# Layer 2's first rows loaded and normalized among the last sums of layer 1

## The chip, the cores and the metric

The kernel runs on one core of one Trainium2 chip. The metric is the device time of one execution in microseconds. The engines are named as in the profile: PE (TensorE: matmuls and transposes, PEld its weight loads), DVE (VectorE), ACT (ScalarE), POOL (GpSimd) and SP (SyncE, which here only issues DMAs). Each engine executes its own queue in order and waits on semaphores; a DMA issued by an engine stands in that engine's queue like any other instruction, so that an issue that has to wait holds back what stands behind it.

## The reference

```python
x = A_x                                   # (1, 2048, 640) fp32
x = x + _A_ref(_layernorm(x), A_wqkv, A_wo)
x = x + _B_ref(_layernorm(x), dft_seq_re, dft_seq_im, dft_hid_re, dft_hid_im)
x = x + _A_ref(_layernorm(x), A_wqkv, A_wo)
x = x + _B_ref(_layernorm(x), dft_seq_re, dft_seq_im, dft_hid_re, dft_hid_im)

def _A_ref(x, wqkv, wo):                  # 32 heads of 20 columns
    q, k, v = split((x @ wqkv))           # no masks, no biases
    p = softmax(q @ k.T * 20 ** -0.5)
    return (p @ v).reshape(1, 2048, 640) @ wo

def _B_ref(x, Cs_re, Cs_im, Ch_re, Ch_im):   # real part of a DFT over both axes
    a, b = x @ Ch_re.T, x @ Ch_im.T
    return Cs_re @ a - Cs_im @ b
```

A layer is attention with its residual sum, then the Fourier block with its own; there are two layers with the same weights.

## The kernel before, in words

All matrices are fp32; a product of two fp32 matrices is made of three matmuls of high and low parts. `split` (L110 to L115) makes them: ACT writes the high part (L114), DVE the low part as the difference (L115). `three` (L117) and `passes` (L124) issue the three matmuls. Rows of x are handled in blocks of 128.

The order of the work is written out by hand: a manual schedule, where each engine receives its instructions in the order in which the program text issues them. Memory comes from pools on the left or right side that are opened and closed as the program goes on.

A layer runs through these classes:

- `Qkv`. `load(k)` (L171 to L175) fetches two row blocks, 2k and 2k+1, with DMAs on SP, one for each block for k of 0 and 1, and one for both otherwise. `stats(k)` calls `moments` (L137 to L151): for each of the two blocks two BATCH_NORM_STATS2 and one BATCH_NORM_AGGREGATE on DVE (L145, L146), then four small steps on POOL (L147 to L150), which make scale and bias of the rows. `norm(k)` applies them on ACT (L154), two instructions. `turn(tb)` transposes four row blocks on PE, 20 transposes (L192), and splits them into `xt`. `fetch` (L200) loads a chunk of the weights for queries or keys, `weights` splits it. `prologue` (L262) puts these together, then goes through the four groups of rows: `product` (30 matmuls into `pqk` for queries and 30 for keys), `keep`, `norms`, `value`.
- `Attention` runs over the heads and takes most of the span; `Check`, which looks at the DFT matrices for their symmetries, stands among its work. `Project` multiplies by wo and adds the first residual; it stores the rows to the scratch tensor d_x[0].
- `Fourier`. `accumulate(m)` sums over the sequence ("pacc" matmuls); the rows are folded by symmetry, and the sixteen sums follow `ORDER = (0, 1, 4, 5, 2, 6, 3, 7, 8, ..., 15)`. `hidden(t)`, t from 0 to 7, makes the product along the columns ("phid" matmuls, 18 of them), then the difference and the sum of its two halves (ACT L1150, DVE L1151 and L1152), adds them to the residual rows (L1160, L1161: the lower rows on DVE, the upper ones on POOL), and stores row blocks t and t+8 with one DMA on SP (L1182, called store t below). For t of 0 and 2 some one-row copies on POOL come with it (L1176, L1181). `residual(t)` (L1157) issues the load of those rows on POOL's queue into one of four buffers. In `run` (L1184), hidden(0) to hidden(3) stand behind accumulate(11) to accumulate(14), hidden(4) to hidden(7) behind the last sum; residual(4) to residual(6) follow accumulate(12) to accumulate(14), and residual(7) follows hidden(4), whose buffers and those of the tiles ahead it needs free.

At the change of layers, layer 2's load(k) reads row blocks 2k and 2k+1, and store t of layer 1 writes row blocks t and t+8: load(0) needs stores 0 and 1, load(1) stores 2 and 3, load(2) stores 4 and 5, load(3) stores 6 and 7. In before, all four loads stand on SP behind store 7. In the prologue of before, ACT's order is norm(0), weights' high parts, norm(1), then the transposes' high parts; DVE's order is the statistics of x0 and x1, the weights' low parts, statistics of x2, the transposes' low parts. x0 is the tile that load(0) fills, and so on; the rows of the profile call all of them "xa".

A general path for matrices without the symmetries exists; it is not executed with these inputs.

Of the kernel before, what the change touches and what calls it, by code (L numbers as in the profile page):

```python
# [5 lines left out]
F32 = mybir.dt.float32  # L6
# [12 lines left out]
LAYERS = 2  # L19
ND = D // 128  # L20
# [15 lines left out]
def mha_fnet_kernel(ctx, tc, x_in, wqk, wv, wo, seq, hid, nat_seq, nat_hid, out):  # L36
# [66 lines left out]
    def rows(ap, t, n=1):  # L103
        return ap[t * 128:(t + n) * 128].rearrange("(n p) d -> p n d", p=128)
# [55 lines left out]
    class Qkv:  # L160
# [6 lines left out]
            s.made, s.raw = set(), {}  # L167


        def load(s, k):  # L170

            s.xn[k] = s.room(f"x{k % 4}", [2, D], F32, "xa")
            n = 1 if k < 2 else 2
            for i in range(0, 2, n):
                nc.sync.dma_start(s.xn[k][:, i:i + n], rows(s.src, 2 * k + i, n))  # L175

        def stats(s, k):
            s.rs[k] = moments(s.xn[k], 2, "a")
# [16 lines left out]
                s.xt[tb, dc] = [x[:, 0], x[:, 1]]  # L195
                split(x[:, 0], x[:, 1], p)

        def fetch(s, c, room=None):
            s.raw[c] = (room or s.fill)("wraw", [ND, 128], F32, "wraw")
            nc.sync.dma_start(s.raw[c], wqk[c])  # L200

        def weights(s, w, c, vector):
# [56 lines left out]
            else:  # L259
                A.activation(dst, src, AF.Copy)  # L260

        def prologue(s, vals, xt, fill, room, att):  # L262
            s.xtp, s.fill, s.room = xt, fill, room
# [7 lines left out]
            raw = [vals(f"v{NT - 1 - dc}", [HD], F32, "wvraw") for dc in range(ND)]  # L271
            for dc in range(ND):
                nc.sync.dma_start(raw[dc], wv[dc, :, :HD])
# [12 lines left out]
            s.stats(3)  # L286
            s.wv = fill("wv", [ND, 2, HD], F32R, "wv")
            for dc in range(ND):
                split(s.wv[:, dc, 0], s.wv[:, dc, 1], raw[dc])

            def ones(t):
                s.v[t] = vals(f"v{t}", [H * VW + 12], F32, "v")
# [709 lines left out]
    class Fourier:  # L1002
# [160 lines left out]
        def hidden(s, t):  # L1163
            lo, hi = s.x[t][:, 0], s.x[t][:, 1]
            o = (t % 4) * 128
            s.nb += 2
            p = [bank(f"b{(s.nb + i) % 8 if t >= NQ else 6 + i}", [128, 512], "phid")[:, :HD + 2] for i in range(2)]
# [12 lines left out]
            if t in (0, 2):  # L1180
                G.tensor_copy(hi[0:1], m)  # L1181
            nc.sync.dma_start(pair(s.dst, t), s.x[t])  # L1182

        def run(s):  # L1184
            s.x, s.acc, s.nb = {}, {}, 0
            for i, m in enumerate(s.ORDER):
                tb, ri, q = m // 8, (m // 4) % 2, m % 4
# [3 lines left out]
                s.parts(i + s.AHEAD)  # L1191
                if m in (6, 7, 9, 10):
                    s.middle((6, 7, 9, 10).index(m))
                if 11 <= m < 15:
                    s.hidden(m - 11)
                if m < 8 and ri == 1:
                    s.residual(q)
                elif 12 <= m < 15:
                    s.residual(m - 8)
            for t in range(4, NP):  # L1200
                s.hidden(t)
                if t == 4:
                    s.residual(NP - 1)

        def general(s):

# [47 lines left out]
    def layer(L, src, dst, general):  # L1254

        tag = f"{L}g" if general else f"{L}"
        q = Qkv(tag, src)
        q.flag = near[:, 5 + L:6 + L] if general else near[:, L:L + 1]
        a = Attention(q, tag)
        p = Project(a, src, d_x[0])  # L1260
        f = Fourier(p, d_x[0], dst, check)
        f.tag = tag
        vals, xt = Pool(f"v{tag}"), Pool(f"xt{tag}", "right")
        fill = Pool(f"fill{tag}", "right")
        a.kq = Pool(f"kq{tag}")
        room = Pool(f"pro{tag}")
        banks(f"q{tag}")
        q.prologue(vals, xt, fill, room, a)
        room.close()

        room = a.room = check.room = Pool(f"att{tag}")
        banks(f"a{tag}")
# [15 lines left out]
        if general:  # L1288
            a.general(done, p)
        else:  # L1290
            a.run(done, p, tasks[L])
        room.close()
        a.kq.close()
        vals.close()
# [4 lines left out]
        p.run()  # L1299
        room.close()  # L1300
        p.late.close()
        if not general:
            f.own = Pool(f"four{tag}")
            f.run()
            f.own.close()
        f.keep.close()
        f.late.close()
        if general:
            f.general()

    def layers(general):
        for L in range(LAYERS):
            layer(L, x_in if L == 0 else d_x[1], out if L == LAYERS - 1 else d_x[1], general)

# [74 lines left out]
```

## Time and profile before

| | us |
|---|---|
| three runs | 2577.2, 2580.96, 2582.15 (median 2580.96) |
| the profiled execution | 2581.92 |
| its span | 2580.1 |
| mean granted clock of TensorE | 0.993 |
| PE busy | 2516.4 (98% of the span) |
| ACT busy | 2136.1 (83%) |
| DVE busy | 982.2 (38%) |
| POOL busy | 539.2 (21%) |

The runs are single executions; the profiled one carries the trace. Busy time counts instructions that do work, not waits and issues of DMAs. In a row of the timeline stand the start and the time in microseconds, the engine, the line, the operation, output and inputs, partitions and elements, the count, and in brackets the idle time before it with what ended it. A row of the chain of waits has the start, the time and the piece of work. SPq means SP's DMA queue.

### The profile page before, as it was taken

The page shows a single profiled execution, that of the slowest core. Times are in us where ns is not written, and L with a number is a line of the kernel's source. Part 1 is how long each engine was busy: PE and PEld are TensorE (multiplying, and loading weights), DVE is VectorE, ACT ScalarE, POOL GpSimd, SP SyncE. Part 2 cuts the span into 40 slices and gives each one's busy share as a digit, 9 for nine tenths or more (in the row PEclk, how much of TensorE's full clock was granted, in tenths as well). Part 3 has the DMA queues.
Part 4 walks back from the last instruction along what each step waited for, and adds up shares of the span by engine and source line. Part 5 has one row for each costly group of instructions (what it writes and reads, how often), then busy time and mean ns, then how long its engine had stood idle before and what let it go on. Part 6 is the DMA issues. An engine that isn't in the chain of part 4 may idle for free.

```text
span 2580.1 us, 43634 instructions
## 1 busy us (share of the span) xinstructions
PE 2516.4 (98%) x16350; PEld 1159.2 (45%) x16350; DVE 982.2 (38%) x2081; ACT 2136.1 (83%) x2429; POOL 539.2 (21%) x1068
## 2 busy tenths in 40 slices
PE   7999999999999999999889999999999999999997
PEld 6644444443333332249775444444433333322596
DVE  5244422344333333416662444223332323242275
ACT  5687899988999999975255888999899999999752
POOL 2112111112111111214420221111121111121143
PEclk9999999999999999999989999999999999999999
DMA  4233221222323223326552342222222222133364
GB/s 170 96 96 114 87 86 45 79 96 75 104 67 90 80 88 108 122 88 235 188 182 92 103 127 83 67 61 73 81 81 65 65 61 80 53 87 104 106 241 162
DMA packets 124921, 263.84 MB, mean 102 GB/s; under 512 B 28080, under 2 KB 52432, under 8 KB 124700
## 3 DMA queue, kind: packets, MB, share of 16 engines
q1 hardware_dynamic: 83804, 150.61, 18.1%
q0 software_dynamic: 40896, 110.34, 13.6%
q8 instruction: 132, 2.16, 0.4%
q14 instruction: 89, 0.73, 0.1%
HBM read 176.60 MB, written 84.21 MB: 101 GB/s over the span
## 4 chain that ended last, share of the span: by engine, by line
PE 89%; DVE 4%; DMA 2%; POOL 2%; issue 1%; ACT 1%; SPq 0%; DVEq 0%; ACTq 0%; POOLq 0%
PE acc L494 37%; PE psc L483 27%; PE pqk L127 11%; PE pv L127 6%; PE py L120 2%; PE py L122 2%; PE py L121 2%; PE pn L227 1%; PE ptr L192 1%; DVE of L501 1%; DMA xd<-d_x 1%; DMA craw<-in_seq_dram 1%; POOL xd L1161 0%; DVE ot L508 0%; DVE on L506 0%
## 5 line engine op out<-in xcount | busy, mean ns | idle before, releaser
L486 ACT ACTIVATE e<-psc 128x1024 f32<-128x1024 f32 x2048 | 1937.8, 1122 | 164.5 <-PE psc L483 128.1
L494 PE MATMUL acc<-e,v 128*32 128x512 f32 x8192 | 1061.5, 602 | 3.8 <-DVE of L501 3.3
L483 PE MATMUL psc<-stq,stk 62*128 62x512 f32 x4096 | 815.2, 462 | 4.6 <-ACT e L486 3.0
L483 PEld LDWEIGHTS psc<-stq,stk 62*128 62x128 f32 x4096 | 341.4, 184 | 836.6 <-ACT e L486 789.9
L494 PEld LDWEIGHTS acc<-e,v 128*32 128x32 f32 x8192 | 187.5, 108 | 366.2 <-issue 338.7
L515 POOL DMA_DIRECT2D o<-oh x256 | 131.2, 521 | 989.6 <-DVE oh L510 988.3
L127 PE MATMUL pqk<-xt,wqk 128*128 128x512 f32 x1200 | 317.6, 409 | 6.1 <-DVE top L228 4.4
L127 PEld LDWEIGHTS pqk<-xt,wqk 128*128 128x128 f32 x1200 | 217.7, 190 | 91.7 <-issue 37.3
L501 DVE STREAM_TRANSPOSE of<-acc 128x512 f32<-128x512 f32 x64 | 45.8, 716 | 529.2 <-PE acc L494 529.2
L112 DVE CAST hl<-pqk 128x512 fp32r<-128x512 f32 x64 | 44.2, 691 | 427.4 <-PE pqk L127 427.4
L127 PE MATMUL pv<-wv,xt 128*128 128x320 f32 x960 | 159.8, 317 | 0.0
L127 PEld LDWEIGHTS pv<-wv,xt 128*128 128x128 f32 x960 | 140.9, 188 | 26.0 <-issue 21.5
L515 POOL DMA_DIRECT2D o<-ot x256 | 128.3, 509 | 0.8 <-issue 0.2
L222 POOL DMA_DIRECT2D scrq<-hl x40 | 28.4, 710 | 386.6 <-DVE hl L115 264.2
L726 DVE TENSOR_REDUCE far<-cq 128x1 f32<-128x512 f32 (+5 forms) x169 | 98.6, 584 | 5.7
L120 PE MATMUL py<-wo,o 128*128 128x320 f32 x320 | 99.1, 310 | 1.4 <-DVE xr L908 1.4
L121 PE MATMUL py<-wo,o 128*128 128x320 f32 x320 | 98.6, 308 | 0.0
L122 PE MATMUL py<-wo,o 128*128 128x320 f32 x320 | 98.6, 308 | 0.0
L730 DVE TENSOR_TENSOR cq<-cq 128x512 f32<-128x512 f32 (+4 forms) x166 | 96.3, 580 | 2.7 <-DMA cq<-in_nat_seq_dram 2.4
L222 POOL DMA_DIRECT2D scrk<-hl x40 | 28.0, 701 | 295.2 <-DVE hl L115 249.8
L258 DVE COPY v<-pv 128x320 f32<-128x320 f32 x32 | 15.7, 490 | 183.5 <-PE pv L127 183.5
L228 DVE TENSOR_REDUCE top<-pn 32x1 f32<-32x512 f32 x80 | 53.4, 675 | 30.4 <-PE pn L227 30.4
(193 smaller groups left out, 1749.9 us busy)
## 6 DMA issues: line engine op xcount, KB each, us to landing
cq<-in_nat_seq_dram POOLq DMA_DIRECT2D x64, 512.0 KB, 5.3
scrq<-hl POOLq DMA_DIRECT2D x40, 512.0 KB, 3.2
scrk<-hl POOLq DMA_DIRECT2D x40, 512.0 KB, 3.5
stq<-scrq SPq DMA_DIRECT2D x256, 80.0 KB
stk<-scrk SPq DMA_DIRECT2D x128, 160.0 KB
o<-o SPq DMA_DIRECT2D x16, 1280.0 KB
stq<-scrq SPq DMA_DIRECT2D x256, 40.0 KB
stk<-scrk SPq DMA_DIRECT2D x128, 80.0 KB
```

The lines of the kernel that those rows point to most:

```text
L120: PE.matmul(out_ap, ah, bh, start=start, stop=False)
L121: PE.matmul(out_ap, ah, bl, start=False, stop=False)
L122: PE.matmul(out_ap, al, bh, start=False, stop=stop)
L127: yield lambda i=i, j=j, k=k: PE.matmul(out_ap, a[i], b[j], start=dc == 0 and k == 0, stop=dc == ND - 1 and k == 2)
L222: G.dma_start(s.scr["qk"[k]][c * 128:(c + 1) * 128, :, tb * 512:(tb + 1) * 512], hl.bitcast(F32))
L483: PE.matmul(p[:, i], s.k[g, kc // 8, j][r, kc % 8 * 128:(kc % 8 + 1) * 128], s.q[g, qb, j][r], start=True, stop=True)
L486: A.activation(e, p, AF.Exp, scale=SCALE)
L494: PE.matmul(s.acc[32 * j:32 * j + 32], s.a.v[kc][:, v0:v0 + 32], s.e[n, j // 2][:, j % 2], start=kc == 0, stop=kc == NT - 1, skip_group_ch ...
L501: V.transpose(t0.rearrange("p b c -> p (b c)"), s.acc)
L515: G.dma_start(s.o[k, h * DH:(h + 1) * DH, qb * 512:(qb + 1) * 512], hl[k][32 * j:32 * j + DH])
L726: V.tensor_reduce(to, x, op=OP.max, axis=AX.X, apply_absolute_value=True)
L730: V.tensor_tensor(y, x, y, op=op)
```

## The change

- A generator `Qkv.begin` takes over the first part of the prologue in three steps: it issues load(0), load(1) and the two weight chunks (on SP) and places the raw weights for v; then stats(0) and stats(1); then norm(0) and norm(1). The weight chunks go into the tiles "k3" and "k4" of the attention's pool of keys and queries, x0 and x1 into a pool of their own, `first`.
- `Fourier.run` gets this generator for the next layer: the loads and the statistics are issued behind the last sum and ahead of hidden(4), the normalization behind hidden(5). For that, `keep` is closed there, and the pool `four` is placed on the right side.
- hidden(3) moves from behind accumulate(14) to directly behind hidden(2), ahead of accumulate(14), and uses the banks b0 and b1.
- The rest of the prologue stays where it was. Its load(2) and load(3) are issued on ACT's queue instead of SP's in layer 2 and stay on SP in layer 1. In both layers norm(1) now stands ahead of the weights' splits.

In the built order, SP has layer 2's loads of x0 and x1 and both weight chunks between store 3 and store 4; DVE has the statistics of x0 and x1 ahead of hidden(4)'s sums; POOL has the two chains of scales ahead of hidden(4)'s adds; ACT has norm(0) and norm(1) behind the second tile's copy (hidden(5)), then hidden(6) and hidden(7), load(2), which waits for store 5, load(3), which waits for store 7, and only then the weights' and the transposes' high parts. PE's transposes of x0 and x1 stand directly behind hidden(7).

```diff
-        def load(s, k):
+        def load(s, k, queue=nc.sync):
-            s.xn[k] = s.room(f"x{k % 4}", [2, D], F32, "xa")
+            s.xn[k] = (s.first if k % 4 < 2 else s.room)(f"x{k % 4}", [2, D], F32, "xa")
...
-                nc.sync.dma_start(s.xn[k][:, i:i + n], rows(s.src, 2 * k + i, n))
+                queue.dma_start(s.xn[k][:, i:i + n], rows(s.src, 2 * k + i, n))
...
+        def begin(s, first, kq, vals):
+            s.first = first
             for k in range(2):
                 s.load(k)
-            s.fetch(0)
-            s.fetch(ND, room)
+            s.fetch(0, kq, "k3")
+            s.fetch(ND, kq, "k4")
+            s.wvraw = [vals(f"v{NT - 1 - dc}", [HD], F32, "wvraw") for dc in range(ND)]
+            yield
+            for k in range(2):
+                s.stats(k)
+            yield
+            for k in range(2):
+                s.norm(k)
+            yield
+
+        def prologue(s, vals, xt, fill, room, att, begin):
+            s.xtp, s.fill, s.room = xt, fill, room
+            next(begin, None)
             for k in (2, 3):
-                s.load(k)
+                s.load(k, nc.sync if s.src is x_in else nc.scalar)
...
-            s.stats(0)
-            s.norm(0)
-            s.stats(1)
+            for _ in begin:
+                pass
             for k in range(2):
                 s.weights(w[k], k * ND, False)
-            s.norm(1)
             s.stats(2)
             s.turn(0)
...
-        def run(s):
+        def run(s, after):
...
-                if 11 <= m < 15:
+                if 11 <= m < 14:
                     s.hidden(m - 11)
+                if m == 13:
+                    s.hidden(3)
...
+            s.keep.close()
+            after = after()
+            for _ in range(2):
+                next(after, None)
             for t in range(4, NP):
                 s.hidden(t)
                 if t == 4:
                     s.residual(NP - 1)
+                elif t == 5:
+                    next(after, None)
...
+    class Start:
+        def __init__(s, L, src, general):
...
+            s.vals, s.a.kq, s.first = Pool(f"v{tag}"), Pool(f"kq{tag}"), Pool(f"first{tag}")
+            s.begin = s.q.begin(s.first, s.a.kq, s.vals)
...
-            f.own = Pool(f"four{tag}")
-            f.run()
+            f.own = Pool(f"four{tag}", "right")
+            f.run(after)
             f.own.close()
```

More of the change, by code (lines that the diff above doesn't have):

```diff
@@ L1166, in hidden @@
             s.nb += 2
-            p = [bank(f"b{(s.nb + i) % 8 if t >= NQ else 6 + i}", [128, 512], "phid")[:, :HD + 2] for i in range(2)]
+            p = [bank(f"b{(s.nb + i) % 8 if t >= NQ else i if t == 3 else 6 + i}", [128, 512], "phid")[:, :HD + 2] for i in range(2)]
             for ri in range(2):
@@ L1262, in layer @@
         f.tag = tag
-        vals, xt = Pool(f"v{tag}"), Pool(f"xt{tag}", "right")
-        fill = Pool(f"fill{tag}", "right")
-        a.kq = Pool(f"kq{tag}")
+        xt, fill = Pool(f"xt{tag}", "right"), Pool(f"fill{tag}", "right")
         room = Pool(f"pro{tag}")
         banks(f"q{tag}")
-        q.prologue(vals, xt, fill, room, a)
+        q.prologue(vals, xt, fill, room, a, start.begin)
         room.close()
+        start.first.close()
         room = a.room = check.room = Pool(f"att{tag}")
@@ L1290, in layer @@
         else:
-            a.run(done, p, tasks[L])
+            a.run(done, p, tasks)
         room.close()
@@ L1301, in layer, with after @@
         p.late.close()
-        if not general:
-            f.own = Pool(f"four{tag}")
-            f.run()
+        if general:
+            f.keep.close()
+            f.late.close()
+            f.general()
+        else:
+            f.own = Pool(f"four{tag}", "right")
+            f.run(after)
             f.own.close()
[L1306 to L1309, printed above, removed]
+            f.late.close()
     def layers(general):
+        todo = [Start(0, x_in, general)]
+        next(todo[0].begin)
         for L in range(LAYERS):
-            layer(L, x_in if L == 0 else d_x[1], out if L == LAYERS - 1 else d_x[1], general)
+            last = L == LAYERS - 1
+            def after():
+                if last:
+                    return iter(())
+                todo.append(Start(L + 1, d_x[1], general))
+                return todo[-1].begin
+            layer(todo[L], d_x[1] if L else x_in, out if last else d_x[1], general, tasks[L], after)
+            if general and not last:
+                next(after())
     layers(False)
```

22 lines of the change are left out of this document (10 added, 12 removed).

## The prediction

> **What bounds the kernel now.** I read the head of the page and its chain of waits first, then the windows over the change of layers, then the chain and the timeline there.
>
> ```profile
> span 2580.1 us, 43634 instructions
> PE 2516.4 (98%) x16350; PEld 1159.2 (45%) x16350; DVE 982.2 (38%) x2081; ACT 2136.1 (83%) x2429; POOL 539.2 (21%) x1068
> PE 89%; DVE 4%; DMA 2%; POOL 2%; issue 1%; ACT 1%; SPq 0%; DVEq 0%; ACTq 0%; POOLq 0%
> ```
>
> PE is busy for 98% of the span and holds 89% of the chain, so a change that leaves the matmuls as they are can only win where PE stands idle. The windows (busy us of PE, PEld, DVE, ACT, POOL, then the granted clock, the DMA share and GB/s) show where that is:
>
> ```profile
> 1260.00:1270.00 10.00, 10.00 (x57) 8.74 (x57) 4.88 (x10) 0.88 (x2) 8.37 (x10) 1.00 0.60 201
> 1270.00:1280.00 10.00, 10.00 (x62) 8.91 (x61) 7.82 (x15) 2.44 (x5) 6.30 (x8) 1.00 0.83 271
> 1280.00:1290.00 10.00, 2.85 (x20) 2.58 (x18) 5.01 (x10) 0.88 (x2) 5.20 (x6) 0.85 0.89 303
> 1290.00:1300.00 10.00, 1.43 (x3) 0.55 (x4) 6.38 (x16) 4.61 (x6) 2.72 (x8) 0.50 1.02 379
> 1300.00:1310.00 10.00, 10.00 (x44) 8.88 (x45) 9.21 (x23) 7.96 (x15) 3.59 (x22) 0.79 0.48 168
> ```
>
> PE works 4.3 of the 20 us from 1280 to 1300; those 15.7 us are all that the change can go after. The chain (start, us, who) says what fills them:
>
> ```profile
> 1267.91 0.72 POOL xd L1181
> 1268.64 2.81 DMA d_x<-xd
> ...
> 1278.32 6.37 DMA xd<-d_x
> ...
> 1284.82 1.05 POOL xd L1160
> 1285.87 1.07 POOL xd L1161
> 1286.95 0.36 SPq L1182
> 1287.41 4.04 DMA xa<-d_x
> 1291.47 0.90 DVE ast L145 x2
> 1292.39 0.21 DVE amv L146
> ...
> 1298.32 1.64 ACT xa L154 x2
> 1300.00 3.88 PE ptr L192 x17
> 1303.88 7.02 PE pqk L127 x30
> 1310.91 2.36 PE ptr L192 x20
> ```
>
> The last residual load (6.37) ends in POOL's adds and in store 7 at 1286.95. All of layer 2's loads stand behind that store on SP, so only then come the load (4.04), statistics, normalization, transposes, and at 1303.88 the stream of 30 pqk matmuls at 7.02/30 = 0.234 us. That stream is the yardstick: behind it PE has no hole left.
>
> **Part by part, at the change of layers.** hidden(3) goes ahead of accumulate(14), whose nine matmuls are 9 x 0.234 = 2.1 us. POOL, though, is in hidden(2)'s copies until 1267.91 + 0.72 = 1268.6, and then needs its two adds:
>
> ```profile
> 1270.53 0.92 POOL L1160 TENSOR_TENSOR xd<-xd,r 128x321 f32<-128x321 f32 x1 [1.24 <-DVE r L1152]
> 1271.41 1.12 POOL L1161 TENSOR_TENSOR xd<-xd,r 128x319 f32<-128x319 f32 x1
> ```
>
> That is 2.0 us (1270.53 to 1272.53), so store 3 is issued at about 1270.65, 1.9 earlier than the 1272.53 of before. Row blocks 0 to 3 are what stores 0 to 3 write, and the second half of x1 waits for store 3 to land. A store's landing is not shown alone but for the 2.81 above; the load's 4.04 bounds it on the other side. I take 3.6, nearer the upper one since the DMA share is 0.83 here: the last half of x1 is issued at 1274.25. By then store 3, two residual loads and x0, x1 have to pass: 0.655 x (1 + 2 + 2) = 3.28 MB. At the 379 GB/s of the row at 1290 that is 8.65 us.
>
> ```profile
> 1290.85 0.95 SPq L175 DMA_DIRECT2D xa<-d_x  x2
> ```
>
> Counted from 0.95 behind store 3's issue (two issues on SP, as in this row), x1 has landed at 1271.6 + 8.65 = **1280.3**. The ends: 1278.3 if only the 4.04 of a load counts, 1282.0 if the raw weights queued behind (two chunks, 0.655 MB, 1.7 us) share the way.
>
> Here is the price. DVE executes in order, and the statistics of x0 and x1 stand in its queue ahead of hidden(4)'s sums. Before, those came at
>
> ```profile
> 1275.38 0.49 DVE L1151 TENSOR_TENSOR r<-phid,r 128x322 f32<-128x322 f32 x1 [1.40 <-ACT r L1150]
> ```
>
> Now they wait for 1280.3 plus one row block's statistics, 0.90 + 0.21 = 1.1: 1281.4, **6.0 late**. Queued behind on DVE are hidden(5) to hidden(7); POOL is held too, since the two small chains of the row scales stand ahead of hidden(4)'s adds:
>
> ```profile
> 1293.69 0.22 POOL L147 TENSOR_SCALAR ars<-amv 128x2 f32<-128x2 f32 x1 [6.76 <-DVE amv L146]
> ...
> 1295.11 0.19 POOL L150 TENSOR_TENSOR ars<-ars 128x2 f32<-128x2 f32 x1
> ```
>
> One chain is 1.6 us (1293.69 to 1295.30), so POOL is at hidden(4) at 1283.0 and done 2.0 later. Only behind these adds does POOL issue residual(7), at 1285.1 instead of 1278.32 (+6.8). Its landing is 5.7 by the median of the view of DMA issues, 6.37 in the chain above:
>
> ```profile
> xd<-d_x POOLq DMA_DIRECT2D x16, 640.0 KB, 5.7
> ```
>
> With 5.7 and the adds' 1.05 + 1.07, store 7 is issued at 1285.1 + 5.7 + 2.1 = **1292.9** against 1286.95. DVE's own share, four tiles of some 2.3 us (from the first sum at 1275.38, 0.49 each, and the adds), ends at about 1290.5 and is hidden under that.
>
> What is gained: x0 and x1 are normalized long before (the 1.64 of ACT at 1298.32 leaves the path), and their 20 transposes (17 of them 3.88) run while store 7 lands. But loads 2 and 3 now stand on ACT's queue, the second one waiting for store 7's landing, and behind it on ACT are the weights' high parts and the copies of the transposes. So ACT stands still until 1292.9 + 3.6 = 1296.5, issues (0.48), and then come:
>
> ```profile
> 1296.97 1.35 ACT L114 ACTIVATE wqk<-wraw 128x640 fp32r<-128x640 f32 x2
> ...
> 1297.73 1.56 DVE L115 TENSOR_TENSOR wqk<-wraw,wqk 128x640 fp32r<-128x640 f32 x2 [1.95 <-ACT wqk L114]
> ...
> 1302.85 0.69 DVE L115 TENSOR_TENSOR xt<-ptr,xt 128x512 fp32r<-128x512 f32 x1 [0.16 <-ACT xt L114]
> ```
>
> First weight on ACT 0.7 (half of 1.35), both low parts on DVE 1.56: 1299.3. In DVE's queue stand next the statistics of x2, 2 x 1.11 = 2.2, then the first low part of the transposes, 0.69: the second pqk matmul starts at 1302.2. Before it started at 1303.88 + 0.23 = 1304.1: **-1.9**. x2 itself waits only for store 5 and is there by then (store 5 near 1288, then 3.6 and a load's 4.04: 1295.6).
>
> The clock takes that back. Before, the stream came right behind the transposes:
>
> ```profile
> 1300.69:1304.10 3.41, 3.41 (x16) 3.33 (x16) 2.96 (x6) 2.38 (x5) 1.34 (x4) 0.50 0.05 17
> ```
>
> This window has a clock of 0.50 and holds transposes but for two matmuls at its end, and the stream after it runs at full rate (7.02 for 30). In the changed kernel the transposes are long over and PE has stood still when the stream begins, so it starts at half rate, as it did here:
>
> ```profile
> 218.57 3.68 PE L127 MATMUL pqk<-xt,wqk 128*128 128x512 f32 x8 [2.24 <-DVE top L228]
> ```
>
> 0.46 us each instead of 0.234. From the window's length of 3.4 us, a full one has passed after 3.4 to 6.8 us, on average 5.1: eleven matmuls at +0.23 are +2.5 (ends +1.7 and +3.4). Boundary: -1.9 + 2.5 = **+0.6**. The Trainium skill, "TensorE: Matmul & The Clock Gate", "Part 4: PE-mode transpose", says that transposes do not count as a busy PE for the clock. The row at 1300.69 speaks against it, since the clock opened behind transposes alone; by the page the stream of before would be cold as well, the 2.5 would fall on both kernels, and the sum below would be -1.5 instead of +1.0.
>
> **Part by part, elsewhere.** Layer 1's start runs through the same code with its norm(1) now ahead of the weights on ACT:
>
> ```profile
> 12.00 0.90 POOL L149 TENSOR_SCALAR ars<-amv 128x2 f32<-128x2 f32 x1
> 12.98 0.62 POOL L150 TENSOR_TENSOR ars<-ars 128x2 f32<-128x2 f32 x1
> 13.64 1.73 ACT L154 ACTIVATE xa<-xa,ars 128x640 f32<-128x640 f32 x2 [1.05 <-POOL ars L150]
> ```
>
> Those two POOL steps took 0.24 and 0.19 in the next chain; without DVE's splits beside them norm(1) starts up to 1.1 earlier, 12.5, and ends 14.3. Weights follow (1.35, low part to about 16.5), x2's statistics 2.2, the first low part 0.7: 19.4. Before, the stream's second matmul stood at about 19.5, behind transposes. So -0.2 at best, up to +1 for queueing and up to +1.7 for a later opening of the clock: ends -0.2 and +2.7, I take +0.8, near the best end because the transposes still run close ahead. At the very end:
>
> ```profile
> 2563.05 7.16 DMA xd<-d_x
> ```
>
> the last load of layer 2 meets less traffic, hidden(3) and its store being 1.9 earlier: between 0 and 7.16 - 6.37 = -0.8, taken as -0.4. The attention, the projection and the sums over columns keep their instructions, and the pools' places cost nothing that a row could show: 0.
>
> **Sum.** +0.6 + 0.8 - 0.4 = **+1.0**, on the profiled execution's 2581.92 us (span 2580.1 and 1.8 around it). That execution is 1.0 above the median of 2580.96, so 2582.9 there is **2582.0** on the median's footing. A difference of 0.2% is 5.2 us, about what a measurement of this kernel can tell from none (its three runs lie 4.95 apart): faster is below 2575.8, slower above 2586.1.
>
> **The rivals.**
>
> *The early rows cost hidden(4) nothing* (faster). If x0 and x1 land before DVE wants hidden(4)'s sums, store 7 goes out at 1286.95 as before, lands 1290.6, and the stream's second matmul is due 5.9 earlier than I have it, 1296.3; PE then stands still for less long, the half rate costs about 2.4, and the boundary gives 1296.3 - 1304.1 + 2.4 = -5.4, in all -5.0, and -6.0 with the start at its good end: 2575 to 2576, on the edge of what counts as faster. It decides at x1's landing by 1274.3 (1275.38 less 1.1). For it: DMA was only 0.60 busy from 1260 to 1270. Against: x1's last half is issued at 1274.25 by my own count. A mix of the good ends gets nearly as far: x1 at 1278.3 (-2.0), clock at its good end (-0.8), start -1.0, tail -0.4: 2577.8. Chance 0.15.
>
> *Two cold or late prologues* (slower). Each microsecond that x1 lands behind 1280.3 moves hidden(4), residual(7), store 7 and the stream by one. From 1284.3 on the whole is more than 5.2 slower. Price: landing at 1285, because the four residual and row loads in flight share the engines with three stores and the weights, gives +4.7 + 1.0, about +6; the half rate over the whole stream of 30 (30 x 0.23 = 6.9 instead of 2.5) gives +4.4 more on its own, +5.4; the start at its bad end adds 1.9. About 2588. For it: DMA share 0.83 to 1.02 here, and DVE, POOL and ACT each wait in order for something of another engine. Against: 379 GB/s was reached in the busiest window. Chance 0.22.
>
> *The clock counts no transposes.* Then the stream of before would be as cold, the 2.5 falls on both, and the sum is -1.5: 2579.5. The full rate of that stream speaks against it; 0.03 of the forecast's chance, and no change of side.
>
> *It does not do what it says.* The loads might stand behind store 7 after all; but in the built order SP has them between store 3 and store 4. If they landed late anyway, that is the case above.
>
> **How the numbers follow.** The forecast has 0.63, the faster case 0.15, the slower 0.22. Eight in ten reach from the good case, 2576, to the bad one, 2588; the forecast's own range, from its terms' ends, is 2577.8 to 2586. Faster 0.15, same 0.63, slower 0.22.
>
> **What would show it.** Right: BATCH_NORM_STATS2 around 1279 to 1281 ahead of hidden(4)'s sums, which start at about 1281.4; residual(7) near 1285; store 7 near 1293; an empty ACT until 1296.5; pqk matmuls of 0.46 for some 5 us. Wrong: sums of hidden(4) still at 1275 or 1276, or a store 7 before 1288 (then faster), or x1 landing after 1284 (then slower), or a stream at full rate from its start.

## The result: 8.0 us slower, and where they are lost

The changed kernel takes 2588.13 us (median of 9 runs, 2585.01 to 2590.28), the kernel before 2580.15 (9 runs, 2576.39 to 2582.28). The ratio is 1.0032, with a 95% interval of 1.0022 to 1.0043. The forecast was 2582.0, +1.0, with a range that ended at 2586. The profiled execution took 2586.92 us, with a span of 2585.0.

The windows of the changed kernel, to be laid beside those of before (busy us of PE, PEld, DVE, ACT, POOL, then clock, DMA share, GB/s):

```profile
1270.00:1280.00 10.00, 10.00 (x60) 8.63 (x59) 5.01 (x7) 2.44 (x5) 2.92 (x4) 1.00 0.88 298
1280.00:1290.00 10.00, 4.18 (x29) 3.91 (x27) 7.39 (x19) 3.90 (x5) 5.24 (x11) 0.94 0.43 162
1290.00:1300.00 10.00, 3.98 (x20) 3.74 (x20) 6.42 (x9) 0.44 (x1) 5.46 (x7) 0.67 0.89 282
1300.00:1310.00 10.00, 1.25 (x2) 0.75 (x3) 4.59 (x11) 3.79 (x7) 0.82 (x2) 0.50 1.02 382
1310.00:1320.00 10.00, 9.55 (x44) 7.73 (x44) 8.86 (x23) 7.75 (x15) 4.39 (x32) 0.86 0.14 48
```

PE's hole was 15.7 us between 1280 and 1300. It is now 20.6 us between 1280 and 1310 (30 less 4.18, 3.98 and 1.25). DVE's row for 1270 to 1280 names the reason: 5.01 us busy instead of 7.82, though it has the statistics added. It stands still and waits for rows. Its timeline:

```profile
1269.59 2.28 DVE L1171 TENSOR_TENSOR xd<-xd,r 128x321 f32<-128x321 f32 x1
...
1279.14 0.89 DVE L145 BATCH_NORM_STATS2 ast<-xa 128x6 f32<-128x320 f32 x2 [3.82 <-DMA xa<-d_x]
...
1282.60 0.89 DVE L145 BATCH_NORM_STATS2 ast<-xa 128x6 f32<-128x320 f32 x2 [2.33 <-DMA xa<-d_x]
...
1283.69 0.89 DVE L145 BATCH_NORM_STATS2 ast<-xa 128x6 f32<-128x320 f32 x2
...
1284.73 0.83 DVE L145 BATCH_NORM_STATS2 ast<-xa 128x6 f32<-128x320 f32 x2
...
1285.73 0.44 DVE L1162 TENSOR_TENSOR r<-phid,r 128x322 f32<-128x322 f32 x1
```

The last row is hidden(4)'s first sum, at 1285.73 instead of 1275.38. Its product was ready long before (the copy on ACT starts at 1276.24, below); DVE idled 3.82 and 2.33 us for the two halves of x0. x1's halves came about a microsecond apart behind it: the last was there when DVE came to it at 1284.73 (its semaphore counts full at 1284.5 in the trace). The chain of waits takes it from there:

```profile
1273.31 9.26 DMA xa<-d_x
1282.60 0.90 DVE ast L145 x2
...
1289.45 6.36 DMA xd<-d_x
1295.95 1.05 POOL xd L1171
1297.00 1.07 POOL xd L1172
1298.08 5.82 DMA d_x<-xd
1304.00 8.67 DMA xa<-d_x
...
1316.87 1.74 ACT xa L154 x2
1318.66 2.08 PE ptr L192 x17
```

Residual(7) is issued at 1289.45 (before 1278.32), store 7 at 1298.08 (before 1286.95). ACT waits for its landing, 5.82, before it may issue the load of x3, and everything that stands behind this on ACT waits too (the row that begins with ACTq holds both loads, x2's at 1297.51 and x3's at 1304.00):

```profile
1297.51 6.86 ACTq L175 DMA_DIRECT2D xa<-d_x  x2
1304.57 1.36 ACT L114 ACTIVATE wqk<-wraw 128x640 fp32r<-128x640 f32 x2 [12.24 <-DMA wvraw<-in_wv_dram]
1306.47 0.79 PE L127 MATMUL pqk<-xt,wqk 128*128 128x512 f32 x1 [10.11 <-ACT xt L114]
1309.54 8.35 PE L127 MATMUL pqk<-xt,wqk 128*128 128x512 f32 x29 [2.28 <-DVE xt L115]
```

ACT idles 12.24 us. (The row names a load of other weights as the releaser; on ACT's own queue stands the load of x3 just ahead, issued at 1304.) The second pqk matmul runs at 1309.5, against 1304.1 before.

A yardstick for the change of layers, used below: from the copy of hidden(4)'s product on ACT to the first pv matmul, behind which PE has no hole left.

```profile
1276.24 0.44 ACT L1161 ACTIVATE r<-phid 128x322 f32<-128x322 f32 x1 [1.88 <-PE phid L122]
...
1321.20 9.07 PE L127 MATMUL pv<-wv,xt 128*128 128x320 f32 x60
```

```profile
1274.91 0.44 ACT L1150 ACTIVATE r<-phid 128x322 f32<-128x322 f32 x1 [1.88 <-PE phid L122]
...
1313.74 9.06 PE L127 MATMUL pv<-wv,xt 128*128 128x320 f32 x60
```

The first pair is of the changed kernel, the second of the kernel before: **44.96 against 38.83 us, +6.1**. The rest of the +7.5 at the first pv matmul lies ahead: 0.55 from layer 1's start, 0.8 in layer 1's Fourier block. These 1.3 us are there already at hidden(4)'s copy (1276.24 against 1274.91), and in the other kernels of this document that copy stands anywhere from 1275.0 to 1277.3, so they are no sure part of the loss. The two spans are only 4.9 apart. Of the 2.6 between that and the +7.5, some 1.8 are a stretch that the profiled execution of before lost to the clock later on and the other did not; the remaining 0.8 lie behind it:

```profile
1380.00:1384.00 4.00, 3.99 (x14) 2.57 (x13) 0.00 (x0) 1.48 (x3) 0.00 (x0) 0.67 0.57 193
```

Here before has a clock of 0.67. In the changed kernel, where the same work stands some 7 us later, the clock is 1.00 from 1376 to 1391. Such stretches differ from run to run, so the medians (8.0 apart) are the fairer measure.

### The profile page after: what moved, and what is told of

It is laid out like the page before. It is cut to its first block, busy times and chain, and to the rows that moved or that the text cites. A ratio compares the mean times of both kernels' runs of the same rounds, so it can differ in the third digit from the quotient of the medians.

```text
span 2585.0 us, 43637 instructions
## 1 busy us (share of the span) xinstructions
PE 2515.4 (97%) x16350; PEld 1157.6 (45%) x16350; DVE 983.3 (38%) x2081; ACT 2135.6 (83%) x2429; POOL 537.9 (21%) x1068
## 4 chain that ended last, share of the span: by engine, by line
PE 88%; DVE 5%; DMA 3%; issue 1%; POOL 1%; ACT 1%; SPq 0%; DVEq 0%; ACTq 0%; POOLq 0%
PE acc L505 37%; PE psc L494 27%; PE pqk L127 11%; PE pv L127 6%; PE py L120 2%; PE py L122 2%; PE py L121 2%; PE pn L227 1%; DVE of L512 1%; DMA xa<-d_x 1%; DMA xd<-d_x 1%; PE ptr L192 0%; DMA craw<-in_seq_dram 0%; DVE ot L519 0%; POOL o L526 0%
## 5 line engine op out<-in xcount | busy, mean ns | idle before, releaser
L258 DVE COPY v<-pv 128x320 f32<-128x320 f32 x32 | 15.7, 490 | 183.4 <-PE pv L127 183.4
```

## The experiments

Theory (order): DVE and POOL work in order, so the statistics of late rows ahead of hidden(4)'s sums hold residual(7), store 7 and all that hangs on it. Rivals: the early loads crowd the DMA engines, whatever the order (traffic); ACT's wait for store 7 is what costs (ACT); the move of hidden(3); store 3's landing. In the table, each ratio is to runs of the kernel before on the same chip (medians 2578.84 to 2581.13), and "layers" is the yardstick above, from the kernel's profiled execution. The ratio is not the quotient of two medians: f5's median lies 2.9 us below that of before, its ratio gives 0.8. And the yardstick holds some luck with the clock: in the changed kernel, e2, e3, e4, e5 and e6, where the pqk stream begins at half rate, its last 29 matmuls took between 8.2 and 9.8 us.

| kernel | us | ratio to before, 95% | layers, us |
|---|---|---|---|
| before | 2580.15 | | 38.83 |
| changed | 2588.13 | 1.0032 (1.0022 to 1.0043) | 44.96 |
| e1_sums_first | 2579.35 | 1.0000 (0.9991 to 1.0009) | 36.92 |
| e2_loads_sp | 2583.66 | 1.0012 (1.0003 to 1.0021) | 42.57 |
| e3_hidden3_back | 2587.92 | 1.0032 (1.0020 to 1.0045) | 47.75 |
| e4_start_back | 2586.64 | one run | 44.07 |
| e5_rows_of_input | 2585.84 | 1.0029 (1.0020 to 1.0039) | 45.54 |
| e6_behind_hidden4 | 2583.36 | 1.0012 (1.0002 to 1.0021) | 41.40 |
| f1_reordered | 2582.55 | 1.0010 (1.0000 to 1.0019) | 40.32 |
| f2_warm | 2581.06 | 1.0009 (1.0000 to 1.0018) | 40.05 |
| f3_fifth | 2582.17 | 1.0009 (1.0000 to 1.0018) | 41.35 |
| f4_norm3_first | 2582.35 | 1.0010 (1.0001 to 1.0019) | 37.75 |
| f5_last_and_sp | 2578.28 | 0.9997 (0.9988 to 1.0006) | 36.02 |
| f6_weights_later | 2577.77 | 0.9988 (0.9979 to 0.9997) | 35.50 |

**e1_sums_first: all statistics behind the sums.**

```diff
-            for _ in range(2):
-                next(after, None)
+            next(after, None)
             for t in range(4, NP):
                 s.hidden(t)
                 if t == 4:
                     s.residual(NP - 1)
-                elif t == 5:
-                    next(after, None)
+            for _ in range(2):
+                next(after, None)
```

> Theory (order): DVE's statistics of x0 and x1 wait for late loads and hold hidden(4)'s sums, so store 7 is late by 11 us and everything that hangs on it. With statistics and norms of x0 and x1 behind hidden(7), and the loads as early as in the changed kernel, hidden(4)'s sums are back near 1277, residual(7) is issued near 1280, store 7 near 1289, the second pqk matmul starts near 1299 to 1301 (1309.5 in the changed kernel, 1304.1 before); total 2576 to 2581. Rival (traffic): the early loads crowd residual(7) and the stores, whatever DVE does first: the sums start near 1277, but store 7 goes out after 1292 and the stream starts after 1304; total 2583 to 2587.

2579.35 us, 8.8 below the changed kernel and no different from before. hidden(4)'s sums, residual(7) and the rest, in the timeline:

```profile
1276.68 0.49 DVE L1162 TENSOR_TENSOR r<-phid,r 128x322 f32<-128x322 f32 x1 [1.40 <-ACT r L1161]
1279.62 0.72 POOL L1168 DMA_DIRECT2D xd<-d_x  x1
1288.09 1.04 POOL L1171 TENSOR_TENSOR xd<-xd,r 128x321 f32<-128x321 f32 x1 [3.01 <-DMA xd<-d_x]
1302.28 6.88 PE L127 MATMUL pqk<-xt,wqk 128*128 128x512 f32 x29 [1.66 <-DVE xt L115]
```

The sums are back at 1276.7, the residual load at 1279.6, and with that the whole loss is gone: it hangs on this order. (The edit moves three things behind hidden(7): DVE's statistics, POOL's scales and ACT's norms; e6 below moves the statistics and scales alone, by one tile.) But the load issued at 1279.62 now takes 8.3 us to land instead of 6.4, so store 7 goes out near 1290 and the stream starts 1 to 3 us later than expected. That is the traffic's share. The yardstick is 1.9 below that of before, and yet no gain shows in the time.

**e6_behind_hidden4: the statistics one tile later only.**

```diff
-            for _ in range(2):
-                next(after, None)
+            next(after, None)
             for t in range(4, NP):
                 s.hidden(t)
                 if t == 4:
                     s.residual(NP - 1)
+                    next(after, None)
                 elif t == 5:
                     next(after, None)
```

> The changed kernel with the statistics of x0 and x1 moved by one tile only: behind hidden(4) and the issue of residual(7), still ahead of hidden(5). If the delay of residual(7)'s issue is the whole cost, store 7 is back near 1290 to 1291 and the total at 2579 to 2581, as with all statistics last. If DVE's and POOL's own queue behind late rows counts too, hidden(5) to hidden(7) start at 1286 and store 7 comes at 1292 to 1294: total 2581 to 2584.

2583.36, a ratio of 1.0012 instead of 1.0032: some five of the eight microseconds are gone, and the rest is what the second reading had. hidden(4) and residual(7) are on time (1276.3 and 1279.2), but hidden(5) waits behind the rows, and ACT still behind store 7:

```profile
1285.10 0.44 DVE L1162 TENSOR_TENSOR r<-phid,r 128x322 f32<-128x322 f32 x1
...
1291.80 8.49 ACTq L175 DMA_DIRECT2D xa<-d_x  x2
1300.50 1.36 ACT L114 ACTIVATE wqk<-wraw 128x640 fp32r<-128x640 f32 x2 [10.98 <-DMA wvraw<-in_wv_dram]
```

**e2_loads_sp: load(2) and load(3) on SP.**

```diff
-                s.load(k, nc.sync if s.src is x_in else nc.scalar)
+                s.load(k)
```

> Only load(2) and load(3) of layer 2 go back to SP's queue, behind store 7. Rival (ACT): what costs is that ACT waits for store 7's landing with the weights' and transposes' high parts behind it; then the high parts are done by 1300 and the stream starts some 5 us earlier, total 2582 to 2584. Theory (order): store 7 is as late as before this edit (near 1298), and on DVE the statistics of x2, whose load needs a store that is no earlier, stand ahead of the transposes' low parts, so the stream moves by 2 us at most: total 2585 to 2589.

2583.66, within what the rival gave and below what the theory gave: ACT's wait costs some 4 us (2.4 of the yardstick) on top of the late store 7. So about half of the loss needs both, the order on DVE and POOL and the loads on ACT. The high parts of the transposes were ready some 5 us earlier, but the low parts still stood behind x2's statistics, as the chain in the second part shows. ACT still idles 6.77 us there, until a store has landed (first row): only some 5 us of its 12.24 were the wait for x3's load.

```profile
1298.81 1.36 ACT L114 ACTIVATE wqk<-wraw 128x640 fp32r<-128x640 f32 x2 [6.77 <-DMA d_x<-xd]
```

```profile
1298.30 4.94 DMA xa<-d_x
1303.24 0.02 issue
1303.26 0.90 DVE ast L145 x2
...
1305.99 9.33 PE pqk L127 x29
```

**e3_hidden3_back: hidden(3) behind accumulate(14) again.**

The product also goes back to the banks 6 and 7.

```diff
-            p = [bank(f"b{(s.nb + i) % 8 if t >= NQ else i if t == 3 else 6 + i}", [128, 512], "phid")[:, :HD + 2] for i in range(2)]
+            p = [bank(f"b{(s.nb + i) % 8 if t >= NQ else 6 + i}", [128, 512], "phid")[:, :HD + 2] for i in range(2)]
...
-                if 11 <= m < 14:
+                if 11 <= m < 15:
                     s.hidden(m - 11)
-                if m == 13:
-                    s.hidden(3)
```

> hidden(3) goes back behind accumulate(14). Theory (order, with store 3's landing as what the last early load waits for): store 3 is issued up to 2 us later, x1 lands, and hidden(4), store 7 and the stream come, as much later: total 2588 to 2591. Rival (hidden(3)'s move costs more than it brings, since its adds ran beside POOL's and store 3 came only at 1272.3): store 3 near 1273 as in the kernel before, total 2585 to 2588.

2587.92, just below the theory's range and inside the rival's; by time nothing moved. In the profiled execution, the slowest of the six, the yardstick grew by 2.8, of which 1.3 is the stream at half rate (29 matmuls in 9.68 us instead of 8.35). The run does not tell whether the move pays; it shows that the move isn't the loss.

**e4_start_back: layer 1's start as before.**

```diff
-            for _ in begin:
-                pass
+            if s.src is x_in:
+                s.stats(0)
+                s.norm(0)
+                s.stats(1)
+            else:
+                for _ in begin:
+                    pass
             for k in range(2):
                 s.weights(w[k], k * ND, False)
+            if s.src is x_in:
+                s.norm(1)
```

> Layer 1's start with norm(1) behind the weights' splits, as in the kernel before; layer 2 unchanged. In the trace the changed kernel is 0.55 us late from its first scores on. If the new order of ACT there is the cause, the second pqk matmul stands at 19.2 to 19.5 and the transposes of the second group at 26.7 as before, and the 0.55 is gone: time about 2587.5; otherwise the 0.55 stays.

One run: 2586.64. It does not settle the 0.55: in this execution the first transposes ran at 15.92 instead of 10.56, with everything behind them, for a reason outside the edit: the first statistics, on which they wait, are late already. Over the other runs with the changed start the matmul reached behind it lies from 0.6 us ahead of before to 1.0 behind, so what the new order costs there stays open, at under a microsecond.

**e5_rows_of_input: the early loads without a wait for stores.** It reads x0 and x1 from the input, so the stores of layer 1 need not have landed.

```diff
-                queue.dma_start(s.xn[k][:, i:i + n], rows(s.src, 2 * k + i, n))
+                queue.dma_start(s.xn[k][:, i:i + n], rows(x_in if k < 2 else s.src, 2 * k + i, n))
```

> The changed kernel, but layer 2's load(0) and load(1) read the rows of the input x instead of layer 1's result, so they need no landing of stores 0 to 3; all the rest, DVE's order too, stays. (The first rows of layer 2's attention are wrong for that.) Theory: with the wait for store 3 gone, the last early load is issued near 1275 instead of 1278.4, lands near 1281, hidden(4)'s sums start near 1284 and not at 1285.7, and the total falls by 1 to 3 to 2585 to 2587, still slower than before since DVE's order is what costs. Rival (store 3's landing is the cause): hidden(4)'s sums back below 1280 and a total of 2578 to 2582.

2585.84, not told apart from the changed kernel. The four loads are issued within 3.54 us instead of 5.92, and yet hidden(4)'s sums come 9.2 us behind their copy (1275.43), against 9.5:

```profile
1271.98 3.54 SPq L175 DMA_DIRECT2D xa<-in_x_dram  x4
...
1284.65 0.44 DVE L1162 TENSOR_TENSOR r<-phid,r 128x322 f32<-128x322 f32 x1
```

So the landing of store 3, on which my prediction hung the last load, is not what makes the rows late: without it they gain 0.3 us. What is left is the time of the transfers themselves, with all that is under way beside them.

**f1_reordered: an attempt at a better order.** Statistics of x0 behind hidden(6) and of x1 behind hidden(7), scales behind hidden(7)'s adds, loads 2 and 3 on SP, in layer 2 the weights ahead of the norms and x2's statistics behind the low parts. (The lines that split `moments` into statistics and scales are left out.)

```diff
-                s.load(k, nc.sync if s.src is x_in else nc.scalar)
+                s.load(k)
...
+            if s.src is x_in:
+                s.norm(0)
+                s.norm(1)
             for k in range(2):
                 s.weights(w[k], k * ND, False)
-            s.stats(2)
+            if s.src is x_in:
+                s.stats(2)
+            else:
+                s.norm(0)
+                s.norm(1)
             s.turn(0)
+            if s.src is not x_in:
+                s.stats(2)
             s.norm(2)
...
-            for _ in range(2):
-                next(after, None)
+            next(after, None)
             for t in range(4, NP):
+                if t == 7:
+                    next(after, None)
                 s.hidden(t)
                 if t == 4:
                     s.residual(NP - 1)
-                elif t == 5:
-                    next(after, None)
+            for _ in range(2):
+                next(after, None)
```

> Early loads as in the changed kernel; DVE's statistics of x0 stand behind hidden(6), those of x1 behind hidden(7); POOL's two scale chains behind hidden(7)'s adds; ACT takes the weights' high parts ahead of the two norms; load(2) and load(3) on SP behind store 7; statistics of x2 behind the transposes' low parts. Theory (order): nothing of layer 2 stands ahead of store 7's chain, store 7 near 1290 as with all statistics last, and what stood behind x2's load (the low parts) no longer does: second pqk matmul near 1297, second transposes near 1305 (1310.8 before), total 2572 to 2577. Rival (traffic): the memory transfers that start early crowd the rest, x2 and x3 come after 1300 and norm(3) holds the second transposes to 1309 or later: total 2578 to 2582.

2582.55, just above the rival's range, though not by its mechanism: x2 and x3 had landed before 1300 (their semaphores count full at 1295.5 and 1299.1). The stream ran from 1299.75, then PE waited for the second group:

```profile
1291.76 1.36 ACT L114 ACTIVATE wqk<-wraw 128x640 fp32r<-128x640 f32 x2 [7.35 <-DMA d_x<-xd]
...
1310.58 0.47 PE L197 MATMUL ptr<-ident,xa 128*128 128x128 f32 x1 [3.24 <-ACT xa L159]
```

The weights' split waited until a store had landed (7.35 us of idle ACT, the norms behind it): their tile lies in memory that a residual tile had, and x2's statistics, put behind the low parts, made the norms of x2 and x3 late.

**f2_warm: PE kept busy.** Against f1, ahead of layer 2's first transposes:

```diff
+                p = s.bank([128, 512], "warm")
+                for _ in range(115):
+                    PE.matmul(p[:, :160], ind[:, :4].rearrange("p a b -> p (a b)"),
+                              ind.rearrange("p a b -> p (a b)"), start=True, stop=True)
             s.turn(0)
```

> The same with 115 small bf16 matmuls (128x128 weights, 160 columns, into a bank that nobody reads) on PE ahead of the first transposes, to keep PE busy while store 7 lands. If PE's half rate at the stream's start costs 1.5 to 2.5 us, as the step of the prediction has it, the pqk stream runs at 0.23 each from its start and the kernel is 1.5 to 2.5 faster than without them; if the second group's rows end last, the gain is 0 to 0.5; 1 or more slower if they hold the transposes.

2581.06; the two intervals overlap, so no gain is shown. Nor could this run have shown the price of the half rate: f1's stream already ran at full rate (first row), and in both the second group of rows ended last. The stream of f2 (second row) was slower than f1's. The small matmuls ended 1.5 us ahead of the transposes, and the transposes came thinly at first; the clock fell (0.50 in the last row), later than in f1, and so was low for longer into the stream:

```profile
1299.75 7.09 PE L127 MATMUL pqk<-xt,wqk 128*128 128x512 f32 x30
```

```profile
1299.75 8.09 PE L127 MATMUL pqk<-xt,wqk 128*128 128x512 f32 x30
```

```profile
1291.80:1295.20 3.40, 1.10 (x9) 0.52 (x6) 1.56 (x2) 3.40 (x5) 1.25 (x3) 0.98 0.81 271
1295.20:1298.60 3.40, 2.86 (x12) 2.57 (x13) 0.95 (x2) 2.32 (x5) 0.00 (x0) 0.50 1.01 369
```

**f3_fifth: a fifth buffer for residual(7), issued behind residual(6).** Against f1:

```diff
-            s.x[t] = s.own(f"x{t % 4}", [2, D], F32, "xd")
+            s.x[t] = s.own(f"x{t % 4}" if t < 7 else "u0", [2, D], F32, "xd")
...
                     s.residual(m - 8)
+                if m == 14:
+                    s.residual(NP - 1)
...
-                if t == 4:
-                    s.residual(NP - 1)
```

> The reordered kernel, and residual(7) goes into memory of the first half's folded sums (a fifth buffer), issued right behind residual(6) instead of behind hidden(4)'s adds. If the wait for that load sets store 7, store 7 comes 2 to 3 us earlier (1287) and x2, x3 with it: total 1 to 3 below the reordered kernel. If the three residual loads and the row loads share the memory's bandwidth, x0 and x1 land 1 to 2 later and the gain is 0.

2582.17, no gain over f1. As the second reading had it, x1 landed some 2 us later (by the trace's semaphores, counted from hidden(4)'s copy). And residual(7) no longer ended last: hidden(7)'s adds on POOL were now released by DVE's sums, which stand behind x0's statistics:

```profile
1288.11 0.93 POOL L1186 TENSOR_TENSOR xd<-xd,r 128x321 f32<-128x321 f32 x1 [2.15 <-DVE r L1178]
```

**f4_norm3_first.** f1 with the norms ahead of the weights, x2's statistics ahead of the low parts, and norm(3) ahead of the split of wv (these lines are against the changed kernel):

```diff
+            s.norm(0)
+            s.norm(1)
             for k in range(2):
                 s.weights(w[k], k * ND, False)
             s.stats(2)
             s.turn(0)
             s.norm(2)
             s.stats(3)
+            if s.src is not x_in:
+                s.norm(3)
...
-                    if tb == k == 0:
+                    if tb == k == 0 and s.src is x_in:
                         s.norm(3)
```

> The reordered kernel once more: norm(0) and norm(1) ahead of the weights on ACT, the statistics of x2 ahead of the transposes' low parts again, and norm(3) ahead of the split of wv. In the reordered kernel the second transposes waited for norm(3) until 1310.6 with the pqk stream over at 1306.7. If norm(3) behind the wv split is what ends last there, the second transposes start near 1307 to 1308 and the total is 2575 to 2579; if x2's load is late, the low parts wait for it and the total stays at 2580 to 2583.

2582.35, though the second transposes ran at 1309.14 without a wait. Two things took the gain. The keeping of the pqk products, now behind the wv split, ended last, and the pv block waited 2.03 us for it. And the clock: the stream's last 29 matmuls took 8.77 us here (all 30 of f1's took 7.09), and the pv block 10.62 instead of 9.06, with a clock of 0.50 in its first 3.4 us:

```profile
1314.66 10.62 PE L127 MATMUL pv<-wv,xt 128*128 128x320 f32 x60 [2.03 <-DVE hl L225]
```

```profile
1314.81:1318.22 3.41, 3.41 (x14) 3.41 (x15) 3.27 (x9) 1.74 (x2) 2.72 (x8) 0.50 0.41 141
```

**f5_last_and_sp: e1 and e2 together.**

> Two edits of the changed kernel together: statistics and norms of x0 and x1 behind hidden(7), and load(2), load(3) on SP behind store 7. With the first alone, load(2) left ACT only at 1295.4, x2 landed at 1299.5 and its statistics held the low parts. If the two costs add up as the theory (order, then ACT's wait) says, x2 lands 2 to 3 us earlier, the pqk stream starts near 1300 and the second transposes end 1.5 to 2.5 earlier than with the first alone: total 2576.5 to 2579. If not, 2579 to 2582, no better than the kernel before.

2578.28, within the expected range and with the stream at 1300.2 as expected, but with an interval that holds no change against before. The yardstick is 0.9 below e1's.

**f6_weights_later: f5 with the two weight chunks behind store 6.** Against f5:

```diff
+            s.wvraw = [vals(f"v{NT - 1 - dc}", [HD], F32, "wvraw") for dc in range(ND)]
+            if s.src is not x_in:
+                yield
             s.fetch(0, kq, "k3")
             s.fetch(ND, kq, "k4")
-            s.wvraw = [vals(f"v{NT - 1 - dc}", [HD], F32, "wvraw") for dc in range(ND)]
...
                     s.residual(NP - 1)
+                elif t == 6:
+                    next(after, None)
```

> As the run beside it, and the two weight chunks (0.655 MB) are loaded behind store 6 instead of ahead of store 4. With them early, residual(7) took 8.3 us to land and stores 4 and 5 took 9 and more. If that traffic is what still holds store 7, residual(7) lands in 6.5 to 7, store 7 is 1 to 1.5 earlier and the total 0.5 to 1.5 lower than beside; if the weights then come too late for their split, it is 1 to 2 higher.

2577.77, ratio 0.9988 (0.9979 to 0.9997): the one version whose interval lies below 1, by 3 us. It is one of thirteen that were compared, and the interval ends close to 1, so the gain is likely rather than certain. Against f5 the gain is within the noise, and the reason given for it is not borne out: residual(7) still took 7.3 us to land (7.9 in f5), and store 7 came only 0.2 us earlier.

## Why the prediction was wrong

The path was the forecast's own: statistics in DVE's order ahead of hidden(4), then residual(7), store 7, ACT. e1 shows that the loss hangs on this order. What failed were the sizes of the transfers on that path: the landing of the rows at 1280.3 and the 3.6 us for the landing of store 7. The forecast counted on the clock of the old trace, and the changed trace runs 1.33 us behind it at hidden(4)'s copy, ahead of anything that the early loads can touch. The last column takes that off.

| step | forecast | measured | measured less 1.33 |
|---|---|---|---|
| store 3 issued | 1270.65 | 1272.3 | 1271.0 |
| x1's last half landed | 1280.3 | 1284.5 | 1283.2 |
| hidden(4)'s sums | 1281.4 | 1285.7 | 1284.4 |
| residual(7) issued | 1285.1 | 1289.45 | 1288.1 |
| store 7 issued | 1292.9 | 1298.1 | 1296.8 |
| store 7 landed, x3's load issued | 1296.5 | 1304.0 | 1302.7 |
| second pqk matmul | 1302.2 | 1309.5 | 1308.2 |

Between the second row and the third, the third and the fourth, and the last two, the forecast holds to 0.2 us. Nearly all of the 6.0 us at the end come from three transfers.

**The rows' landing (+2.5).** "3.28 MB at 379 GB/s, 8.65 us" was the step that failed first. From the same point, 0.95 behind store 3's issue, x1's last half took 11.2 us:

```profile
1273.29:1284.49 11.20, 10.89 (x72) 10.62 (x72) 4.83 (x11) 1.95 (x5) 1.31 (x3) 1.00 0.90 342
1272.00:1274.50 2.50, 2.50 (x14) 1.76 (x13) 1.33 (x3) 1.56 (x3) 0.86 (x2) 1.00 0.84 165
1274.50:1282.50 8.00, 8.00 (x55) 8.00 (x55) 1.91 (x5) 0.88 (x2) 0.06 (x1) 1.00 1.01 387
```

At 342 GB/s these are 3.83 MB. So 0.55 MB more passed than I had counted, 1.5 us at 379; they fit the two weight chunks (0.655 MB), which I had left out of the sum and put only into the bad end. The other 1.1 us are the low start, 165 GB/s around the issue of the loads; from then on the rate was 387, even above the 379. The part of the weights is an argument from bytes: no run took them away and left the rest as it was. That the last load waits for store 3 is not the reason. The store took 6.0 us and not 3.6, but e5 did away with the wait and gained 0.3. The Trainium skill, "DMA: Bandwidth & Descriptors", section "Issuing engines are not separate DMA queues", says that transfers issued by different engines run on the same DMA engines and interleave. The trace agrees: x0's second half took 9.26 us with store 3 and two residual loads of another queue beside it, while the first row load of before, of the same size, took 4.04.

**Residual(7)'s landing (+0.8).** It was 6.36, as in the chain of before, and not the median of 5.7; with the steps around it store 7 came 0.8 later.

**Store 7's landing (+2.3).** It was 5.82 and not 3.6. The 3.6 was a guess between 2.81 and 4.04, and the 2.81 is no landing: that piece of the chain ends where a POOL step begins, and the store's semaphore counts full only 3.9 us behind its issue. By the same count the stores of before took 3.1 to 5.2 us.

**Store 3 (+0.4).** It was issued 1.7 later than forecast, 1.3 of it the shift of the trace. With hidden(3) right behind hidden(2), DVE's first add took 2.28 us instead of 0.49, beside three POOL steps (until 1271.5). It counts little, as e5 shows. The Trainium skill, "SBUF — State Buffer", section "SBUF: two separate sides", has DVE steps with two inputs in SBUF and POOL's take turns at one port for whole instructions; the 2.28 row agrees, the add ending 0.4 us behind the third POOL step.

**What then came last.** The stream was no longer the end: x3's load took 8.67 us behind ACT's wait, and norm(3) held the second transposes until 1318.66, which the forecast had as hidden. That is 0.5 us at the first pv matmul.

**What held.** The half rate at the stream's start was there: 29 matmuls in 8.35, some 1.6 us over the full rate, against 2.5 forecast. In the six kernels with such a stream it was 1.4 to 3.0, 2.3 on average, so the 2.5 was a fair size and this execution a lucky one. That transposes count for the clock holds too. The window of before still had two matmuls at its end; in e1 the window 1296.40 to 1299.80 has 15 PE steps, transposes all, at 0.51, and the next window a clock of 1.00:

```profile
1296.40:1299.80 3.40, 3.06 (x15) 2.81 (x15) 1.81 (x3) 3.34 (x6) 0.00 (x0) 0.51 0.94 323
1299.80:1303.20 3.40, 1.74 (x11) 1.29 (x10) 3.33 (x9) 1.10 (x3) 1.15 (x3) 1.00 0.69 206
```

The start was +0.55 against +0.8, though by the spread that e4 shows this is no more than agreement in size; the tail was 0 against -0.4 (7.13 and 7.16). The 0.8 in layer 1's Fourier block, where a load of a DFT chunk ended later, was not foreseen and not followed further.

**The rival that came true** is the slower one, by its mechanism: late rows, everything moved with them. Its mark was a landing of x1 behind 1284.3 (by its own sum, 5.2 less 1.0 behind 1280.3, it is 1284.5). In the trace x1 landed at 1284.5, at 1283.2 without the shift, so the rows alone do not carry the 8.0: the longer landing of store 7, which that rival did not price, makes up the rest.

## What to carry to other kernels

Work that is moved ahead on an engine that executes in order should stand behind the steps of the chain that ends last, and not ahead of them, unless its data have certainly landed: an idle DVE is no reason to give it something to wait for. When several transfers are started in the same few microseconds, count all of them that can be under way, not only those that one waits for, and lengthen every landing on the path: here a store's went from some 3.6 to 5.8 us. And look at what an engine's waiting DMA issue has queued behind it, and in whose memory the new tiles lie: both held ACT here (e2 and f1).

## What the runs showed of the hardware

Three things that I had not expected. One DVE add beside POOL steps took 2.28 us instead of 0.49. The same load of 640 KB landed in 6.4 us in the kernel before and in 8.3 in e1, with 1.97 MB of other loads started ahead of it. And 8 us of small matmuls did not keep PE's clock up over a gap of 1.5 us followed by thin transposes (0.98, then 0.50).
